# A narrower odd matmul for each token pair, its mirror on VectorE and its sum on GpSimd a slot ahead

## The chip, the cores and the metric

The kernel runs on one core of a Trainium2 chip. The metric is the device time of one execution in microseconds; the median of three runs is 424.52 us (424.30 to 424.62).

## The reference

The input x is 8 x 3072 x 256 (f32). It goes through a Fourier mixing (the real part of an FFT over the sequence and the channels) and then through a feed-forward layer whose hidden unit is the maximum of three linear maps:

```python
X = np.fft.fft(np.fft.fft(x, axis=1), axis=2).real          # 8 x 3072 x 256
t = X.reshape(24576, 256)
h = np.maximum(np.maximum(t @ w1, t @ w2), t @ w3)          # 24576 x 768
out = h @ w_out                                              # 24576 x 256, f32
```

The matmuls of the kernel take bf16 and sum in f32.

## The kernel before

**The mathematics used.** The real part of a Fourier transform of real data splits into an even and an odd part, and the tokens come in pairs whose even parts agree and whose odd parts differ in sign (but for one channel row). So each mixed batch is kept as two bf16 matrices, `tE` and `tO`, of 128 rows and 1536 token pairs. One pair yields two tokens, called plus and minus here. The maximum of three maps is written as `w1` plus the larger of two differences and zero, so that the output has a linear part, `tE` and `tO` times the small matrices in `gw`, and a hidden part, `hp` (plus) and `hm` (minus) times `wout_bf`.

**Units.** For each of B = 8 batches there are three blocks of 512 token pairs (`blk`), and in each block six units (`jc`, 128 hidden columns each): 18 units a batch (`UNITS`). A unit does this in program order, and each engine runs its own instructions in that order:

- `unit_plus`: four 512-column matmuls into two PSUM banks (lines 476, 477); `unit_out` evicts them, ScalarE with a relu into `stmp` (line 490) and VectorE with a maximum into `hp` (line 491).
- `finish` of the unit before: `unit_minus`, two 512-column matmuls into that unit's banks (line 484), and again the two evictions, into `hm`. The banks of a unit are thus free two units later.
- `l2_some(10)`: ten steps of the second layer of the block before. A step is one `next()` of a generator, which runs up to its next `yield`, as a rule one matmul.
- the planned pieces of that unit (`plan`): the mixing of the next batch (`s` and `k` pieces, lines 430 to 460), the fetches of x by SyncE's queue, and the casts of x on GpSimd (`turn_chunk`, lines 144 and 146).

After the six units `l2_some(1000)` runs what is left of the generator.

**The second layer.** `l2_block` handles four slots of 128 token pairs. For every two slots the even part goes into a bank `pl` (two 256-column matmuls, line 516) and ScalarE copies it to `even` (line 520). For each slot a bank `po` gets the odd part of both tokens, one 512-column matmul against 512 columns of `gw` (line 524, followed by a second `yield`), then six 256-column matmuls of `hp` in its left half and six of `hm` in its right half (line 500). VectorE then adds the even part to both halves and writes `ot` (line 529). A GpSimd indirect DMA stores the minus half (line 534), SyncE the plus half (line 544). `po` comes from the pool `ps_o`, which has two buffers: slot s+2 takes the bank of slot s once everything that reads it is done. There are 23 such blocks, 92 slots; the last block of the last batch has a function of its own, `l2_last`.

**The weights.** `prep_second` (called through `prep_some`) computes `gw` in unit 5 of the first batch: twelve matmuls into `psw`, a cast by VectorE (line 409) and a scaled copy by ScalarE (line 410).

Of the kernel before, what the change touches and what calls it, by code (L numbers as in the profile page):

```python
# [9 lines left out]
FP32 = mybir.dt.float32  # L10
BF16 = mybir.dt.bfloat16
INT32 = mybir.dt.int32
AX = mybir.ActivationFunctionType
ALU = mybir.AluOpType
# [19 lines left out]
def kernel(  # L34
# [46 lines left out]
    gE = [consts.tile([128, DFF], BF16, name=f"gE{i}", tag=f"gE{i}") for i in range(2)]  # L81
    gO = [consts.tile([128, DFF], BF16, name=f"gO{i}", tag=f"gO{i}") for i in range(2)]
    gD = [consts.tile([128, DFF], BF16, name=f"gD{i}", tag=f"gD{i}") for i in range(2)]
    gw = consts.tile([128, 768], BF16, tag="gw")
    rows_m = consts.tile([128, 12 * B], INT32, tag="rows_m")
    mark = consts.tile([1, 1], FP32, tag="mark")
    sgn = consts.tile([128, 1], FP32, tag="sgn")
    dif = consts.tile([128, 1], FP32, tag="dif")
    t_mid = consts.tile([128, 2, B], BF16, tag="t_mid")
    z_all = consts.tile([128, 128 * 26], BF16, tag="z_all")  # L90
    z = z_all.rearrange("p (c r) -> p c r", r=26)
# [40 lines left out]
                     in_=bass.AP(xs.tensor, xs.offset + (m - 1) * 64 + lo,  # L132
                                 [xs.ap[0], [1, hi - lo], [-64, m]]))

    def turn_chunk(b, ch):

        if ch == 0:
            x0 = x0_pool.tile([96, 66 * 130], BF16, name="x0", tag="x0")
            v = x0.rearrange("p (dl bb) -> p dl bb", bb=130)
            turned[b] = (lambda d: v[:, d, 0:128], rows_back(v[:, 33:66, :]))  # L140
            turned[b, "v"] = v
        v = turned[b, "v"]
        xs = raw.pop((b, ch))
        nc.gpsimd.tensor_copy(v[:, 0:33, ch * 32:ch * 32 + 32],  # L144
                              xs[:, 0:32 * 64].rearrange("p (bb dl) -> p dl bb", dl=64)[:, 0:33, :])
        reverse(lambda out, in_: nc.gpsimd.tensor_copy(out, in_), v[:, 33:66, :], xs,  # L146
                ch * 32, 33 if ch == 3 else 32)

    def rows_back(v):
        return lambda d: v[:, 32 - d, 0:128] if d else v[:, 32, 1:129]  # L150
# [60 lines left out]
    for (name, value) in (("half_pi", 0.5 * math.pi), ("rnd", ROUND), ("n24", -24.0)):  # L211
        c = gen.tile([128, 1], FP32, name=name, tag=name)
        nc.vector.memset(c, value)
        consts_of[name] = c
    nc.vector.memset(z[:, :, 24:26], 0.0)
    nc.vector.memset(m0f[:, 50:52], 0.0)
    nc.vector.memset(m0r[:, 50:52], 0.0)
    half = gen.tile([128, 256], FP32, tag="half")
# [169 lines left out]
    def prep_second():  # L388

        for jp in range(NJC // 2):  # L390
            pst = ps_f.tile([128, 512], FP32, name="pst", tag="ps")
            for k in range(2):
                jc = jp * 2 + k
                for fc in range(2):
                    nc.tensor.matmul(
                        pst[:, k * 256:(k + 1) * 256],
                        w1_bf[:, fc * DFF + jc * 128: fc * DFF + jc * 128 + 128],
                        md[fc], start=(fc == 0), stop=(fc == 1))
            nc.vector.tensor_copy(out=g1t[:, jp * 512:(jp + 1) * 512], in_=pst)
            yield  # L400
        psw = ps_f.tile([128, 512], FP32, name="psw", tag="ps")
        for half in range(2):
            for jc in range(NJC):
                nc.tensor.matmul(
                    psw[:, half * 256:(half + 1) * 256],
                    g1t[:, jc * 256 + half * 128: jc * 256 + half * 128 + 128],
                    wout_bf[:, jc * 256:(jc + 1) * 256],
                    start=(jc == 0), stop=(jc == NJC - 1))
        nc.vector.tensor_copy(out=gw[:, 0:512], in_=psw)
        nc.scalar.activation(out=gw[:, 512:768], in_=psw[:, 256:512], func=AX.Copy, scale=sgn)  # L410
        yield

    class Mix:
# [87 lines left out]
                             start=False, stop=(jc == NJC - 1), skip_group_check=True)  # L501
            yield

    def l2_block(b, blk, hp, hm, te, to):

        base = b * S
        for sub in range(4):
            slot = blk * 4 + sub
            r = slot + 1
            cp = slice(slot * 128, slot * 128 + 128)  # L510
            sp = slice(sub * 128, sub * 128 + 128)
            if sub % 2 == 0:
                pl = ps_f.tile([128, 512], FP32, name="pl", tag="ps")
                for i in range(2):
                    ci = (slot + i) * 128
                    nc.tensor.matmul(pl[:, i * 256:(i + 1) * 256], te[:, ci:ci + 128],  # L516
                                     gw[:, 0:256], start=True, stop=True)
                    yield
                even = even_pool.tile([128, 512], FP32, name="even", tag="even")
                nc.scalar.copy(out=even, in_=pl)  # L520
            lin = even[:, (sub % 2) * 256:(sub % 2 + 1) * 256]
            po = ps_o.tile([128, 512], FP32, name="po", tag="po")
            ot = out_pool.tile([128, 512], FP32, name="ot", tag="ot")
            nc.tensor.matmul(po, to[:, cp], gw[:, 256:768], start=True, stop=True)  # L524
            yield
            yield
            yield from l2_hidden(po[:, 0:256], lambda jc: hp[:, jc, sp])
            yield from l2_hidden(po[:, 256:512], lambda jc: hm[:, jc, sp])
            nc.vector.tensor_tensor(  # L529
                out=ot.rearrange("p (h c) -> p h c", h=2),  # L530
                in0=po.rearrange("p (h c) -> p h c", h=2),
                in1=lin.unsqueeze(1).to_broadcast([128, 2, 256]), op=ALU.add)
            lo = 1 if r == 12 else 0
            stored(nc.gpsimd.indirect_dma_start(  # L534
                out, bass.IndirectOffsetOnAxis(
                    ap=rows_m[0:128 - lo, b * 12 + slot: b * 12 + slot + 1], axis=0),
                ot[lo:128, 256:512], None), "scattered", ("scattered", "direct"))
            nc.gpsimd.memset(mark, 0.0)
            if r <= 11:
                stores = [(0, 128, base + r)]  # L540
            else:
                stores = [(0, 64, base), (64, 128, base + 12)]
            for (p0, p1, row) in stores:
                stored(nc.sync.dma_start(out=out[row: row + 24 * (p1 - p0 - 1) + 1: 24, :],
                                         in_=ot[p0:p1, 0:256]), "direct", ("scattered",))

    def l2_last(hp, hm, te, to, flipped):
# [3 lines left out]
        for sub in (3, 0, 1, 2):  # L551
# [6 lines left out]
            ot = out_pool.tile([128, 512], FP32, name="ot", tag="ot")  # L558
            for (h, tev, tov, wo, hid) in (
                    (0, te[:, cp], to[:, cp], gw[:, 256:512], lambda jc: hp[:, jc, sp]),  # L560
                    (1, ter[:, sm], tor[:, sm], gw[:, 512:768], lambda jc: hm[:, jc, sm])):
                if sub == 2 and h == 1:
                    po = ps_f.tile([128, 512], FP32, name="pol", tag="ps")
                ph = po[:, h * 256:(h + 1) * 256]
                nc.tensor.matmul(ph, tev, gw[:, 0:256], start=True, stop=False)
                yield
                nc.tensor.matmul(ph, tov, wo, start=False, stop=True)
                yield
                yield from l2_hidden(ph, hid)
                if sub == 2:  # L570
                    nc.vector.tensor_copy(out=ot[:, h * 256:(h + 1) * 256], in_=ph)
# [72 lines left out]
    ps_o = ctx.enter_context(tc.tile_pool(name="ps_o", bufs=2, space=bass.MemoryType.PSUM))  # L644
    h_pool = ctx.enter_context(tc.tile_pool(name="hbuf", bufs=2))
    out_pool = ctx.enter_context(tc.tile_pool(name="outbuf", bufs=6))
    even_pool = ctx.enter_context(tc.tile_pool(name="evenbuf", bufs=2))
    second = [prep_first(1, lambda: ps_o.tile([128, 512], FP32, name="psg", tag="po")),
              prep_second()]

# [17 lines left out]
    def at(b, unit, fn):  # L668
        plan.setdefault((b + unit // UNITS, unit % UNITS), []).append(fn)
# [16 lines left out]

    for (u, fn) in ((0, prep_some), (0, prep_some), (1, prep_some), (1, prep_some),
                    (2, lambda: m.k(2)), (2, prep_some), (3, lambda: m.k(3)),
                    (3, prep_some), (4, prep_some), (5, prep_some),
                    (6, lambda: m.k(4)), (7, lambda: m.k(5)), (7, m.end),  # L690
                    (0, lambda: turn_chunk(1, 0)), (2, lambda: turn_chunk(1, 1)),
                    (5, lambda: turn_chunk(1, 2)), (8, lambda: turn_chunk(1, 3))):
        at(0, u, fn)
    for ch in range(4):
        at(0, (6, 7, 9, 11)[ch], lambda ch=ch: fetch(2, ch))
    for b in range(B - 1):
        for i, whats in enumerate(ahead):
            for what in whats:
                at(b, begin[b] + i - (b == 0 and i >= 6), lambda b=b, what=what: piece(b + 1, what))
        if b + 2 < B:  # L700
            folds = begin[b] + 8 if b else 14
            for ch in range(4):
                at(b, folds + (0, 2, 4, 6)[ch], lambda b=b, ch=ch: turn_chunk(b + 2, ch))
                if b + 3 < B:
                    at(b, UNITS + (0, 1, 2, 4)[ch], lambda b=b, ch=ch: fetch(b + 3, ch))

    for b in range(B):
# [15 lines left out]
        for blk in range(3):  # L723
# [7 lines left out]
            for jc in range(NJC):  # L731
# [2 lines left out]
                if prev is not None:  # L734
                    finish(prev)
                prev = (pses, tO[:, cs], jc, hm)
                l2_some(10)
                if b == B - 1 and blk == 0:
                    if jc == 0:
                        middle = l2_mid()  # L740
# [5 lines left out]
            if blk == 2:  # L746
                finish(prev)
            l2_queue.append(l2_last(hp, hm, tE, tO, flipped) if b == B - 1 and blk == 2 else
                            l2_block(b, blk, hp, hm, tE, tO))

    l2_some(1000)

# [28 lines left out]
```

## Time and profile before

| | |
|---|---|
| median of three runs | 424.52 us |
| the profiled execution | 424.57 us, span of the engines 422.8 us |
| granted TensorE clock | 1.00 |
| PE busy | 404.0 us (96%) |
| VectorE (DVE) busy | 276.8 us (65%) |
| ScalarE (ACT) busy | 258.9 us (61%) |
| GpSimd (POOL) busy | 243.8 us (58%) |
| one batch in steady state | 48.45 us (18 units) |

All times are of one execution. A line of the timeline gives the start and the length in us, the engine, the source line, the operation, the output and the inputs, and in brackets how long the engine had been idle and what ended that. A line of the groups gives the count, the busy time in us, the mean length in ns, and the idle time ahead with its cause. Matmuls are pipelined: the length of one is longer than the time to the start of the next, and the spacing of starts is what PE spends on it.

### The profile page before, as it was taken

The numbers are of one execution on the slowest core, as the hardware profiler recorded it, in microseconds if no ns is written. First come the engines' busy times: TensorE is split into PE (matmuls) and PEld (weight loads), VectorE is DVE, ScalarE is ACT, GpSimd is POOL, SyncE is SP. The second block draws the span as 40 slices with busy tenths as digits, with TensorE's granted clock in tenths as the row PEclk, the third lists the DMA queues.
The fourth block names the chain that finished last, engine by engine and source line by source line (L and its number), as shares of the span: only waits on it lengthen the run. The fifth ranks groups of instructions, "written<-read, shape, count | busy, mean of one in ns | idle before, by whom it ended". The sixth has DMA issues, their size and how long they took to land.

```text
span 422.8 us, 8683 instructions
## 1 busy us (share of the span) xinstructions
PE 404.0 (96%) x3028; PEld 270.1 (64%) x3083; DVE 276.8 (65%) x460; ACT 258.9 (61%) x478; POOL 243.8 (58%) x291
## 2 busy tenths in 40 slices
PE   0899999999999999999999999999999999999996
PEld 0365667666676766666676666666666666666665
DVE  8877666566666665675666665675656665666773
ACT  6856666666665666556666666656665566655650
POOL 9927837962479526982299525983289621214420
PEclk9999999999999999999999999999999999999999
DMA  9998895793318831596217841387211221212213
GB/s 107 105 181 179 181 219 143 166 205 85 107 66 204 182 129 43 130 222 125 98 61 187 201 135 51 111 203 174 98 64 64 64 76 64 75 51 54 98 73 128
DMA packets 131172, 51.89 MB, mean 123 GB/s; under 512 B 113073, under 2 KB 128184, under 8 KB 131128
## 3 DMA queue, kind: packets, MB, share of 16 engines
q1 hardware_dynamic: 105408, 35.93, 35.8%
q0 software_dynamic: 24784, 15.08, 16.5%
q8 instruction: 24, 0.39, 0.4%
q10 hardware_dynamic: 936, 0.33, 0.3%
q14 instruction: 20, 0.16, 0.1%
HBM read 29.02 MB, written 25.17 MB: 128 GB/s over the span
## 4 chain that ended last, share of the span: by engine, by line
PE 87%; POOL 4%; DVE 3%; issue 3%; ACT 2%; DMA 1%; DVEq 0%; ACTq 0%; POOLq 0%
PE po L500 28%; PE pse L476 15%; PE pse L484 13%; PE pse L477 12%; PE po L524 4%; POOL x L100 3%; PE ps L458 2%; PE ps L456 2%; PE ps L430 2%; PE pl L516 2%; PE ps L432 2%; ACT stmp L490 1%; DVE ot L529 1%; PE psg L376 1%; DVE hp L491 1%
## 5 line engine op out<-in xcount | busy, mean ns | idle before, releaser
L490 ACT ACTIVATE stmp<-pse 128x512 bf16<-128x512 f32 x288 | 171.6, 600 | 52.0 <-PE pse L477 38.6
L534 POOL DMA_INDIRECT out_dram<-ot,rows_m x92 | 100.3, 1090 | 157.8 <-DVE ot L529 149.7
L491 DVE TENSOR_TENSOR hp<-pse,stmp 128x512 bf16<-128x512 f32 x144 | 99.6, 691 | 126.8 <-ACT stmp L490 87.0
L476 PE MATMUL pse<-t,gE 128*128 128x512 bf16 x285 | 108.1, 379 | 2.2 <-ACT t L460 0.2
L491 DVE TENSOR_TENSOR hm<-pse,stmp 128x512 bf16<-128x512 f32 x144 | 99.2, 689 | 6.8 <-ACT stmp L490 6.7
L477 PE MATMUL pse<-t,gO 128*128 128x512 bf16 x255 | 96.6, 379 | 0.2
L500 PE MATMUL po<-wout_bf,hp 128*128 128x256 bf16 x576 | 86.1, 273 | 0.3
L484 PE MATMUL pse<-t,gD 128*128 128x512 bf16 x274 | 82.7, 379 | 0.4
L500 PE MATMUL po<-wout_bf,hm 128*128 128x256 bf16 x570 | 77.8, 273 | 0.3
L500 PEld LDWEIGHTS <-hp 128*128 128x128 bf16 x576 | 56.3, 98 | 26.2
L500 PEld LDWEIGHTS <-hm 128*128 128x128 bf16 x576 | 56.4, 98 | 16.3
L144 POOL CAST x<-xs 96x1056 bf16<-96x1056 f32 x28 | 56.8, 2028 | 11.0 <-DMA xs<-in_x_dram 11.0
L529 DVE TENSOR_TENSOR ot<-po,even 128x512 f32<-128x512 f32 x92 | 62.9, 684 | 0.0
L146 POOL CAST x<-xs 96x1056 bf16<-96x1056 f32 (+1 forms) x35 | 58.2, 1675 | 0.0
L460 ACT CAST t<-ps 128x512 bf16<-128x512 f32 x47 | 27.5, 585 | 43.3 <-PE ps L458 43.2
L437 ACT CAST z_all<-ps 128x480 bf16<-128x480 f32 x45 | 25.1, 558 | 42.1 <-PE ps L432 42.1
L484 PEld LDWEIGHTS <-gD 128*128 128x128 bf16 x288 | 27.9, 98 | 32.2
L477 PEld LDWEIGHTS <-gO 128*128 128x128 bf16 x288 | 28.1, 98 | 20.3 <-issue 1.5
L476 PEld LDWEIGHTS <-gE 128*128 128x128 bf16 x288 | 28.1, 98 | 19.2 <-issue 0.4
L524 PE MATMUL po<-gw,t 128*128 128x512 bf16 x87 | 33.0, 379 | 0.0
L520 ACT COPY even<-pl 128x512 f32<-128x512 f32 x46 | 26.8, 582 | 0.1
L430 PE MATMUL ps<-m24f,x 96*128 96x96 bf16 x224 | 24.7, 205 | 0.0
(147 smaller groups left out, 328.2 us busy)
## 6 DMA issues: line engine op xcount, KB each, us to landing
xs<-in_x_dram SPq DMA_DIRECT2D x84, 198.0 KB
out_dram<-ot SPq DMA_DIRECT2D x90, 128.0 KB
xs<-in_x_dram SPq DMA_DIRECT2D x28, 192.0 KB
out_dram<-ot,rows_m POOLq DMA_INDIRECT x92, 3.3
x<-in_x_dram POOLq DMA_DIRECT2D x12, 96.0 KB, 4.3
w_bf<-in_moe_w_dram POOLq DMA_DIRECT2D x6, 192.0 KB, 5.5
out_dram<-ot SPq DMA_DIRECT2D x17, 64.0 KB
xs<-in_x_dram SPq DMA_DIRECT2D x32, 5.8 KB
```

The costliest lines, as they stand in the source:

```text
L144: nc.gpsimd.tensor_copy(v[:, 0:33, ch * 32:ch * 32 + 32], xs[:, 0:32 * 64].rearrange("p (bb dl) -> p dl bb", dl=64)[:, 0:33, :])
L146: reverse(lambda out, in_: nc.gpsimd.tensor_copy(out, in_), v[:, 33:66, :], xs, ch * 32, 33 if ch == 3 else 32)
L430: nc.tensor.matmul(ps1[:, c0:c0 + n], x0[0](d), mf[:, 0:n], start=True, stop=False)
L476: nc.tensor.matmul(pse[:, 0:n], gE[i][:, js], te, start=True, stop=False)
L477: nc.tensor.matmul(pse[:, 0:n], gO[i][:, js], to, start=False, stop=True)
L484: nc.tensor.matmul(pse, gD[i][:, js], to, start=False, stop=True, skip_group_check=True)
L490: nc.scalar.activation(out=stmp[:, 0:n], in_=pses[0][:, 0:n], func=AX.Relu)
L491: nc.vector.tensor_tensor(out=dst, in0=src3, in1=stmp[:, 0:n], op=ALU.max)
L500: nc.tensor.matmul(po, hcols(jc), wout_bf[:, jc * 256:(jc + 1) * 256], start=False, stop=(jc == NJC - 1), skip_group_check=True)
L524: nc.tensor.matmul(po, to[:, cp], gw[:, 256:768], start=True, stop=True)
L529: nc.vector.tensor_tensor(out=ot.rearrange("p (h c) -> p h c", h=2), in0=po.rearrange("p (h c) -> p h c", h=2), in1=lin.unsqueeze(1).to_br ...
L534: stored(nc.gpsimd.indirect_dma_start(out, bass.IndirectOffsetOnAxis(ap=rows_m[0:128 - lo, b * 12 + slot: b * 12 + slot + 1], axis=0), ot[ ...
```

## The change

The odd part of a slot is computed for the plus token alone: one matmul of 257 columns, 256 of weights and one that picks row 0 of `tO`. The odd part of the minus token is its negative, but for row 0, which enters with the same sign. VectorE makes this mirror: `other = twice * po[:, 256] - po[:, 0:256]`, where `twice` holds twice the weights' row 0 (with 1 subtracted in column 0, because column 256 of the bank also stays under the minus half). GpSimd adds the even part and leaves a line of 512 values, even | even + other; VectorE's last sum takes it as it is. Even part, odd matmul, mirror and GpSimd's add of a slot are issued while the slot before is being worked on: the odd part between its `hp` and its `hm` matmuls, the even part of a pair between the third and the fourth `hp` matmul of an odd slot. The second `yield` is gone, and `l2_some` takes 10, 9, 9, 10, 9, 9 steps in the units of a block. A new piece of `prep_second` makes `twice` (one matmul, two VectorE operations) and takes a planned place of its own in unit 5. The casts of x are cut into halves (17 and 16 of 33 columns `d`), one to a unit in units 6 to 21 (in batch 0 two to a unit, 14 to 21). `even` has three buffers of double width in place of two.

```diff
@@ turn_chunk
+        for (d0, d1) in (((0, 17), (17, 33))[part % 2:part % 2 + 1] if part is not None else ((0, 33),)):
+            if part is None or part < 2:
+                nc.gpsimd.tensor_copy(v[:, d0:d1, ch * 32:ch * 32 + 32],
+                                      xs[:, 0:32 * 64].rearrange("p (bb dl) -> p dl bb", dl=64)[:, d0:d1, :])
+            if part is None or part >= 2:
+                reverse(lambda out, in_: nc.gpsimd.tensor_copy(out, in_), v[:, 33:66, :], xs,
+                        ch * 32, 33 if ch == 3 else 32, 32 + d0, 32 + d1)
@@ start
+    nc.vector.memset(two_row, 0.0)
+    nc.vector.memset(two_row[0:1], 2.0)
+    nc.vector.memset(gw[:, 512:513], 0.0)
+    nc.vector.memset(gw[0:1, 512:513], 1.0)
@@ prep_second
         nc.vector.tensor_copy(out=gw[:, 0:512], in_=psw)
-        nc.scalar.activation(out=gw[:, 512:768], in_=psw[:, 256:512], func=AX.Copy, scale=sgn)
+        nc.scalar.activation(out=gw[:, 514:770], in_=psw[:, 256:512], func=AX.Copy, scale=sgn)
+        yield
+        pst = ps_f.tile([128, 512], FP32, name="pst", tag="ps")
+        nc.tensor.matmul(pst[:, 0:256], two_row, gw[:, 256:512], start=True, stop=True)
+        nc.vector.tensor_copy(out=twice, in_=pst[:, 0:256])
+        nc.vector.tensor_scalar(out=twice[:, 0:1], in0=twice[:, 0:1], scalar1=-1.0, scalar2=None,
+                                op0=ALU.add)
         yield
@@ second layer
+    def l2_even(b, slot):
+        pl = ps_f.tile([128, 512], FP32, name="pl", tag="ps")
+        for i in range(2):
+            ci = (slot + i) * 128
+            nc.tensor.matmul(pl[:, i * 256:(i + 1) * 256], mixes[b].tE[:, ci:ci + 128],
+                             gw[:, 0:256], start=True, stop=True)
+            yield
+        even = even_pool.tile([128, 1024], FP32, name="even", tag="even")
+        nc.scalar.copy(out=even.rearrange("p (i c) -> p i c", i=2)[:, :, 0:256],
+                       in_=pl.rearrange("p (i c) -> p i c", i=2))
+        for i in range(2):
+            lines[b, slot + i] = even[:, i * 512:(i + 1) * 512]
+
+    def l2_odd(b, slot):
+        po = ps_o.tile([128, 512], FP32, name="po", tag="po")
+        nc.tensor.matmul(po[:, 0:257], mixes[b].tO[:, slot * 128:slot * 128 + 128], gw[:, 256:513],
+                         start=True, stop=True)
+        other = other_pool.tile([128, 256], FP32, name="other", tag="other")
+        nc.vector.scalar_tensor_tensor(out=other, in0=twice, scalar=po[:, 256:257],
+                                       in1=po[:, 0:256], op0=ALU.mult, op1=ALU.subtract)
+        line = lines[b, slot]
+        nc.gpsimd.tensor_tensor(out=line[:, 256:512], in0=line[:, 0:256], in1=other, op=ALU.add)
+        odd[b, slot] = po
+        yield
@@ l2_block
-            po = ps_o.tile([128, 512], FP32, name="po", tag="po")
-            nc.tensor.matmul(po, to[:, cp], gw[:, 256:768], start=True, stop=True)
-            yield
-            yield
-            yield from l2_hidden(po[:, 0:256], lambda jc: hp[:, jc, sp])
+            if (b, slot) not in odd:
+                yield from l2_even(b, slot)
+                yield from l2_odd(b, slot)
+            after = (b, slot + 1) if slot < 11 else (b + 1, 0)
+            lin = lines.pop((b, slot))
+            po = odd.pop((b, slot))
+            first = l2_hidden(po[:, 0:256], lambda jc: hp[:, jc, sp])
+            for _ in range(3):
+                next(first)
+                yield
+            if after < (B - 1, 8) and sub % 2:
+                yield from l2_even(*after)
+            yield from first
+            if after < (B - 1, 8):
+                yield from l2_odd(*after)
             yield from l2_hidden(po[:, 256:512], lambda jc: hm[:, jc, sp])
-            nc.vector.tensor_tensor(
-                out=ot.rearrange("p (h c) -> p h c", h=2),
-                in0=po.rearrange("p (h c) -> p h c", h=2),
-                in1=lin.unsqueeze(1).to_broadcast([128, 2, 256]), op=ALU.add)
+            nc.vector.tensor_tensor(out=ot, in0=po, in1=lin, op=ALU.add)
@@ plan
-                    (3, prep_some), (4, prep_some), (5, prep_some),
+                    (3, prep_some), (4, prep_some), (5, prep_some), (5, prep_some),
...
             for ch in range(4):
-                at(b, folds + (0, 2, 4, 6)[ch], lambda b=b, ch=ch: turn_chunk(b + 2, ch))
+                for part in range(4):
+                    at(b, 6 + 4 * ch + part if b else 14 + 2 * ch + part // 2,
+                       lambda b=b, ch=ch, part=part: turn_chunk(b + 2, ch, part))
@@ unit loop
-                l2_some(10)
+                l2_some(9 + (jc % 3 == 0))
```

More of the change, by code (lines that the diff above doesn't have):

```diff
@@ L83 @@
     gD = [consts.tile([128, DFF], BF16, name=f"gD{i}", tag=f"gD{i}") for i in range(2)]
-    gw = consts.tile([128, 768], BF16, tag="gw")
+    gw = consts.tile([128, 770], BF16, tag="gw")
     rows_m = consts.tile([128, 12 * B], INT32, tag="rows_m")
     mark = consts.tile([1, 1], FP32, tag="mark")
+    two_row = consts.tile([128, 128], BF16, tag="two_row")
     sgn = consts.tile([128, 1], FP32, tag="sgn")
     dif = consts.tile([128, 1], FP32, tag="dif")
+    twice = consts.tile([128, 256], FP32, tag="twice")
     t_mid = consts.tile([128, 2, B], BF16, tag="t_mid")
@@ L133, in reverse, with turn_chunk @@
                                  [xs.ap[0], [1, hi - lo], [-64, m]]))
-    def turn_chunk(b, ch):
-        if ch == 0:
+    def turn_chunk(b, ch, part=None):
+        if (b, "v") not in turned:
             x0 = x0_pool.tile([96, 66 * 130], BF16, name="x0", tag="x0")
@@ L142, in turn_chunk @@
         v = turned[b, "v"]
[L143 to L147, printed above, removed]
+        xs = raw[b, ch]
+        for (d0, d1) in (((0, 17), (17, 33))[part % 2:part % 2 + 1] if part is not None else ((0, 33),)):
[5 more added lines that the diff above has]
+                        ch * 32, 33 if ch == 3 else 32, 32 + d0, 32 + d1)
     def rows_back(v):
@@ L502, in l2_hidden, with l2_block @@
             yield
-    def l2_block(b, blk, hp, hm, te, to):
+    lines = {}
+    odd = {}
+    def l2_even(b, slot):
[21 more added lines that the diff above has]
+        yield
+    def l2_block(b, blk, hp, hm):
         base = b * S
@@ L509, in l2_block @@
             r = slot + 1
-            cp = slice(slot * 128, slot * 128 + 128)
             sp = slice(sub * 128, sub * 128 + 128)
[L512 to L517, printed above, removed]
-                    yield
-                even = even_pool.tile([128, 512], FP32, name="even", tag="even")
-                nc.scalar.copy(out=even, in_=pl)
-            lin = even[:, (sub % 2) * 256:(sub % 2 + 1) * 256]
-            po = ps_o.tile([128, 512], FP32, name="po", tag="po")
-            ot = out_pool.tile([128, 512], FP32, name="ot", tag="ot")
-            nc.tensor.matmul(po, to[:, cp], gw[:, 256:768], start=True, stop=True)
-            yield
-            yield
-            yield from l2_hidden(po[:, 0:256], lambda jc: hp[:, jc, sp])
+            if (b, slot) not in odd:
[4 more added lines that the diff above has]
+            po = odd.pop((b, slot))
+            ot = out_pool.tile([128, 512], FP32, name="ot", tag="ot")
+            first = l2_hidden(po[:, 0:256], lambda jc: hp[:, jc, sp])
[7 more added lines that the diff above has]
+                yield from l2_odd(*after)
             yield from l2_hidden(po[:, 256:512], lambda jc: hm[:, jc, sp])
-            nc.vector.tensor_tensor(
-                out=ot.rearrange("p (h c) -> p h c", h=2),
-                in0=po.rearrange("p (h c) -> p h c", h=2),
-                in1=lin.unsqueeze(1).to_broadcast([128, 2, 256]), op=ALU.add)
+            nc.vector.tensor_tensor(out=ot, in0=po, in1=lin, op=ALU.add)
             lo = 1 if r == 12 else 0
@@ L560, in l2_last @@
                     (0, te[:, cp], to[:, cp], gw[:, 256:512], lambda jc: hp[:, jc, sp]),
-                    (1, ter[:, sm], tor[:, sm], gw[:, 512:768], lambda jc: hm[:, jc, sm])):
+                    (1, ter[:, sm], tor[:, sm], gw[:, 514:770], lambda jc: hm[:, jc, sm])):
                 if sub == 2 and h == 1:
@@ L646 @@
     out_pool = ctx.enter_context(tc.tile_pool(name="outbuf", bufs=6))
-    even_pool = ctx.enter_context(tc.tile_pool(name="evenbuf", bufs=2))
+    other_pool = ctx.enter_context(tc.tile_pool(name="otherbuf", bufs=2))
+    even_pool = ctx.enter_context(tc.tile_pool(name="evenbuf", bufs=3))
     second = [prep_first(1, lambda: ps_o.tile([128, 512], FP32, name="psg", tag="po")),
@@ L700 @@
         if b + 2 < B:
-            folds = begin[b] + 8 if b else 14
             for ch in range(4):
-                at(b, folds + (0, 2, 4, 6)[ch], lambda b=b, ch=ch: turn_chunk(b + 2, ch))
+                for part in range(4):
+                    at(b, 6 + 4 * ch + part if b else 14 + 2 * ch + part // 2,
+                       lambda b=b, ch=ch, part=part: turn_chunk(b + 2, ch, part))
                 if b + 3 < B:
@@ L748 @@
             l2_queue.append(l2_last(hp, hm, tE, tO, flipped) if b == B - 1 and blk == 2 else
-                            l2_block(b, blk, hp, hm, tE, tO))
+                            l2_block(b, blk, hp, hm))
     l2_some(1000)
```

## The prediction

> **What bounds the kernel now.** I read the page first (busy times, slices), then the groups by form, then the timeline of one block in steady state and of the stage at 37 to 43 us, then GpSimd's own timeline.
>
> ```profile
> PE 404.0 (96%) x3028; PEld 270.1 (64%) x3083; DVE 276.8 (65%) x460; ACT 258.9 (61%) x478; POOL 243.8 (58%) x291
> ...
> PE   0899999999999999999999999999999999999996
> ...
> L534 POOL DMA_INDIRECT out_dram<-ot,rows_m x92 | 100.3, 1090 | 157.8 <-DVE ot L529 149.7
> L529 DVE TENSOR_TENSOR ot<-po,even 128x512 f32<-128x512 f32 x92 | 62.9, 684 | 0.0
> ```
>
> PE is never idle after the first 20 us; every other engine has a third of its time free. So a matmul cycle saved is time saved, and a wait put in front of a matmul is time lost in full. The timeline around one unit (four `unit_plus`, two `unit_minus`, then a group of `l2_some` steps, then a planned piece) shows how the engines stand to each other:
>
> ```profile
> 243.48 0.82 PE L500 MATMUL po<-wout_bf,hm 128*128 128x256 bf16 x6
> ...
> 244.56 0.81 PE L476 MATMUL pse<-t,gE 128*128 128x512 bf16 x2
> ...
> 245.42 0.59 PE L484 MATMUL pse<-t,gD 128*128 128x512 bf16 x2
> 245.85 0.69 DVE L491 TENSOR_TENSOR hp<-pse,stmp 128x512 bf16<-128x512 f32 x1 [1.50 <-ACT stmp L490]
> 245.85 0.38 PE L516 MATMUL pl<-gw,t 128*128 128x256 bf16 x2
> ...
> 246.07 0.38 PE L524 MATMUL po<-gw,t 128*128 128x512 bf16 x1
> 246.29 0.82 PE L500 MATMUL po<-wout_bf,hp 128*128 128x256 bf16 x6
> ...
> 246.47 0.69 DVE L491 TENSOR_TENSOR hm<-pse,stmp 128x512 bf16<-128x512 f32 x1
> ...
> 247.08 0.68 DVE L529 TENSOR_TENSOR ot<-po,even 128x512 f32<-128x512 f32 x1
> ```
>
> Three things. A 512-column matmul holds PE 0.22 us (246.07 to 246.29), a 256-column one 0.11 (245.85 to 246.07). With T = 244.56 the unit's l2 steps start at T+1.29. And the sum into `ot` (L529) is late: its last matmul started at 244.03 (243.48 plus five times 0.109), yet it runs at T+2.52 to T+3.20. A generator emits what follows its last yield only at the next call, and when a slot ends on the last step of a group, that call is in the next unit, behind that unit's `hp` and `hm` on VectorE. VectorE was idle 1.50 us meanwhile. Today nobody needs that bank soon: the next slots use the other one.
>
> **The change, part by part.**
>
> Odd part. 92 matmuls go from 512 to 257 columns: 92 x (0.2155 - 0.1095) = 9.75 us off PE.
>
> Steps. A block of l2 now has 56 steps, one matmul each: slot 0 has 13 (odd of slot 1 at step 6), slot 1 steps 13 to 27 (odd of slot 2 at 21), slot 2 steps 28 to 40 (odd of slot 3 at 34), slot 3 steps 41 to 55 (odd of the next block's slot 0 at 49). The groups of 10, 9, 9, 10, 9, 9 take steps 0-9, 10-18, 19-27, 28-37, 38-46, 47-55. Four odd matmuls and four first `hp` matmuls are thus in different units, so the new wait of `hp` for VectorE's mirror is covered: mirror at T+2.52 to T+2.94, `hp` no earlier than the next unit's T+1.29, that is T+3.56 in the shortest unit (6 x 0.2155 + 9 x 0.109 = 2.27 us). Without that cover it would cost about 1 us a slot.
>
> The bank. `ps_o` has two buffers, so odd of slot s+1 overwrites the bank of slot s-1 and must wait for `ot` of s-1. For steps 6, 21 and 49 that `ot` runs half a microsecond or more ahead (the tightest: `ot` of slot 0 ends at T+3.21 of unit 1, odd at T+3.78). For step 34 it doesn't. Slot 1 ends on step 27, the last of the third group, so its `ot` comes out with step 28, in the fourth unit, at T+2.52 to T+3.20 as in the timeline. Odd of slot 3 is due six steps into the same unit: T + 1.29 + 6 x 0.109 = T+1.95. From VectorE's end to PE's start takes 0.05 us in the nearest row (below: `hm` ends at 38.22, the matmul into its bank starts at 38.27), 0.14 at the start (`nat` to PE at 20.12). So PE stands still 3.25 - 1.95 = 1.30 us (1.4 with the longer release), in every block of l2_block: 23 of them. In the first, three extra steps put odd at T+2.27: 0.98. Sum 22 x 1.30 + 0.98 = 29.6 us. Nothing covers it, PE being in order.
>
> The start. The new `pst` matmul stands right behind `psw` and reads `gw`:
>
> ```profile
> 37.53 0.69 DVE L491 TENSOR_TENSOR hm<-pse,stmp 128x512 bf16<-128x512 f32 x1
> ...
> 38.27 0.38 PE L476 MATMUL pse<-t,gE 128*128 128x512 bf16 x1
> ...
> 40.45 0.38 PE L476 MATMUL pse<-t,gE 128*128 128x512 bf16 x1
> ...
> 40.65 0.69 DVE L409 CAST gw<-psw 128x512 bf16<-128x512 f32 x1 [0.21 <-PE psw L404]
> ```
>
> `gw` is done at 41.34; today PE goes on at 40.45, with it at 41.40 + 0.11 = 41.51: 1.06 lost. Slot (0,0) has its mirror and its `hp` in one group: `hm` and mirror end at T+2.94, `hp` is due at T+1.62: 1.37 lost. Together 2.4 us; zero to 3 are the ends. Four memsets (0.06 to 0.17 each) on VectorE ahead of the first loads: 0.1.
>
> VectorE. The mirror (`scalar_tensor_tensor`, 256 columns out of PSUM) isn't in the trace: 425 ns for a 256-column copy out of PSUM (L571) below, 684 for L529 above; nearest the first: 0.42, 39 us in all, in its free third. With 0.68 the units with mirror and `ot` would run 0.2 late, some 2 us over the kernel.
>
> GpSimd. The add of two 128x256 f32 isn't there either. Casts of 1056 and 32 columns (2035 and 234 ns) give 0.18 + 1.76 ns a column: 0.63 for one input of 256, 1.08 for two; the bf16 copy of 512 in 609 gives a lower end near 0.3. I take 0.8. [...] Of a batch's 12 slots GpSimd then has 16 half casts at 1.1 (17.6 plus 0.5 for the short pieces), 12 stores at 0.97 + 0.17 gap, one of them 1.6 longer (15.3), memsets 1.1 and adds 9.6: 44 of the new 51 us (48.45 - 1.28 + 3 x 1.30). It has over 4 us between mirror and need. Batch 0 packs two casts a unit into units 14 to 21; there it falls behind about 4 us, at the edge: 0.2 us, up to 1. Queued behind a late add is `ot` on VectorE, and behind that all `hp`; that is the price if the cover goes.
>
> The spread casts and the strided `even` copy change no wait: x is fetched in a batch's units 0 to 4, the DMA engines are back under half load 25 us after the first fetch (246 of 221 us), and its casts stand in units 6 to 21, each chunk's 14 us or more behind its fetch.
>
> Sum, against the profiled execution's 424.57 (span 422.8, and within 0.05 of the median): 424.57 - 9.75 + 29.6 + 2.4 + 0.1 + 0.2 = 447.1.
>
> **Rivals.** (1) The bank is free in time, because `ot` of slot 1 is emitted a step earlier than I count or the bank's release isn't where I see it. Then 447.1 - 29.6, and with shorter blocks GpSimd's lag in batch 0 costs some 1.2 and VectorE's margins 0.5: 419. It decides by one step: at 27 steps or fewer for the first two slots the sum runs within the third unit, T+2.87 to T+3.56, before odd at the fourth's T+1.95 (= T+4.22). For it speaks that no matmul waits for L529 today; against it that L534's 149.7 us of waiting come from exactly these late sums. Chance 0.13. (2) GpSimd binds: from an add of (51 - 34.5) / 12 = 1.38 us on, each 0.1 more costs 1.2 us a batch for six batches; at 1.6 it gives 447 + 16 = 463. Above my upper end: 0.04. (3) The stalls make PE slow afterwards. At the start PE's first 27 matmuls last 479 ns on average, later ones of that size 379; at such a price after each of 23 stalls, 23 x 27 x 0.1 = 62 us: 509. The granted clock reads 1.00 through the stops at 24 to 42 us; 0.02. [...] (4) 257 columns cost as 512: 457; against it the spacing of 0.042 at 96, 0.109 at 256, 0.216 at 512. 0.02.
>
> **Numbers.** Forecast 447.1, chance 0.79, own range 443.5 to 451.5 (release 0.05 to 0.14, start 0 to 3, mirror and add at their ends). For eight in ten I put 442 to 454. Slower by over 0.2% (about what a measurement of this kernel can tell): 0.79 + 0.04 + 0.02 + 0.02 = 0.87; faster 0.12 from rival 1; 0.01 between.
>
> **What would show it.** In the profile after: about 23 PE stops of 1.0 to 1.4 us, three a batch, each before the 257-column matmul and ended by VectorE's `ot`, some 30 us in the waits; PE busy near 394 us, a batch in about 51 us rather than 48.45; 1.1 us of PE waiting for `gw` near 41 us and 1.4 for the first mirror; POOL adds under 1.1 us. Wrong if PE has no such stops, if `ot` of slot 1 runs before the fourth unit's `hp`, or if the stops stand before `hp` matmuls instead.

## The result and the profile after

| | median, us | ratio to before |
|---|---|---|
| before | 424.59 | |
| after | 455.03 (454.5 to 457.4) | 1.0719 (1.0705 to 1.0733) |
| forecast | 447.1, range 442 to 454 | |

The change makes the kernel slower, as forecast, but by 30.4 us and not by 22.5; the time lies 1 us above the range. The profiled execution is the slowest of the five (457.38 us, span 455.6). Its page, first the busy times, PE's slices and the clock granted to PE in each slice (tenths), then the groups that answer to those shown of before, with the odd matmul added:

```profile
PE 404.8 (89%) x3084; PEld 270.9 (59%) x3084; DVE 313.4 (69%) x558; ACT 259.4 (57%) x478; POOL 317.1 (70%) x431
...
PE   0779889889889889889889889889889889889886
...
PEclk9979999999999999999999999999999999999999
...
L575 POOL DMA_INDIRECT out_dram<-ot,rows_m x92 | 103.2, 1122 | 82.7 <-DVE ot L573 75.1
...
L573 DVE TENSOR_TENSOR ot<-po,even 128x512 f32<-128x512 f32 x92 | 62.6, 681 | 3.1 <-POOL even L545 2.8
...
L539 PE MATMUL po<-gw,t 128*128 128x257 bf16 x92 | 25.3, 275 | 27.3 <-DVE ot L573 27.3
```

PE's slices run 9, 8, 8 to the end: two 8s in every three slices of 11.4 us, which is two blocks of 17 us, so a stop comes back with every block. The last group names it: PE waits 27.3 us ahead of the 257-column matmul, for `ot`. The second and third slices are 7s, and in the third the granted clock reads 7 tenths: the start is slower as well. (PE's busy time doesn't fall to the 394 us of the forecast: a stop counts as idle only from the modelled end of the matmul ahead, 0.16 us after the next could start, part of the start runs at half the clock (0.50 from 25 to 30 us), and 55 of before's records of matmuls were missing.)

The timeline of the unit that holds the stop answers to the one shown of before:

```profile
250.72 0.38 PE L491 MATMUL pse<-t,gE 128*128 128x512 bf16 x1
...
251.98 0.69 DVE L506 TENSOR_TENSOR hp<-pse,stmp 128x512 bf16<-128x512 f32 x1 [0.55 <-PE pse L499]
252.01 0.82 PE L515 MATMUL po<-wout_bf,hp 128*128 128x256 bf16 x6
...
252.62 0.69 DVE L506 TENSOR_TENSOR hm<-pse,stmp 128x512 bf16<-128x512 f32 x1
253.23 0.68 DVE L573 TENSOR_TENSOR ot<-po,even 128x512 f32<-128x512 f32 x1
253.97 0.28 PE L539 MATMUL po<-gw,t 128*128 128x257 bf16 x1 [1.14 <-DVE ot L573]
254.09 0.49 PE L515 MATMUL po<-wout_bf,hm 128*128 128x256 bf16 x3
```

T is 250.72. The six `hp` matmuls start at T+1.29; the odd matmul of slot 3 is due at 252.66 (T+1.94) and starts at 253.97, 0.06 us behind the end of slot 1's `ot` (253.91): 1.31 us lost. The bracket says 1.14, because it counts from the modelled end of the last `hp` matmul. One batch takes 51.13 us (first `hp` of batch 4 at 245.66, of batch 5 at 296.79).

The start, VectorE's timeline, before and then after. Before:

```profile
12.26 1.11 DVE L131 COPY back<-x 96x1056 bf16<-96x1056 bf16 x1
```

After:

```profile
18.76 1.15 DVE L133 COPY back<-x 96x1056 bf16<-96x1056 bf16 x1 [3.91 <-DMA x<-in_x_dram]
```

The first x arrives late, and the first unit's `hp` runs at 36.02 us where it ran at 27.73. PE's timeline shows two losses on the way. The first matmuls of the mixing, before:

```profile
20.12 0.20 PE L430 MATMUL ps<-m24f,nat 96*128 96x96 bf16 x1 [0.15 <-DVE nat L316]
20.16 0.20 PE L432 MATMUL ps<-m24r,back 96*128 96x96 bf16 x1
```

And after:

```profile
26.14 0.24 PE L445 MATMUL ps<-m24f,nat 96*128 96x96 bf16 x1 [5.64 <-DVE nat L325]
...
26.26 0.28 PE L445 MATMUL ps<-m24f,nat 96*128 96x96 bf16 x1
26.34 0.28 PE L447 MATMUL ps<-m24r,back 96*128 96x96 bf16 x1
```

PE waits 5.64 us for the copies of x and starts the mixing 6.0 us later. Then it goes at half its pace, 0.08 us a matmul instead of 0.042, up to 30.9 us: the clock granted from 25 to 30 us is 0.50, where it was 1.00. That is the other 2.3 us of the 8.3. No step of the forecast had either loss. The change doesn't touch the loads of x, but its new tiles stand among the constants, ahead of the tiles of x: in the built program the first tile of x lies at byte 62464 of a partition before (a multiple of 512) and at 63776 after (32 past a multiple of 256).

### The profile page after: what moved, and what is told of

Read it like the earlier page. It is cut to its first block, busy times and chain, and to the rows that moved or that the text cites. A ratio compares the mean times of both kernels' runs of the same rounds, so it can differ in the third digit from the quotient of the medians.

```text
span 455.6 us, 9096 instructions
## 1 busy us (share of the span) xinstructions
PE 404.8 (89%) x3084; PEld 270.9 (59%) x3084; DVE 313.4 (69%) x558; ACT 259.4 (57%) x478; POOL 317.1 (70%) x431
## 4 chain that ended last, share of the span: by engine, by line
PE 66%; DMA 9%; issue 6%; DVE 6%; SPq 5%; ACT 4%; POOL 4%; DVEq 0%; ACTq 0%; POOLq 0%
PE po L515 21%; PE pse L491 11%; PE pse L492 10%; PE pse L499 10%; DMA xs<-in_x_dram 6%; SPq L102 5%; DVE ot L573 4%; ACT stmp L505 3%; PE po L539 3%; DMA x<-in_x_dram 2%; PE pl L527 2%; PE ps L445 2%; PE ps L447 2%; PE ps L473 2%; PE ps L471 2%
## 5 line engine op out<-in xcount | busy, mean ns | idle before, releaser
L575 POOL DMA_INDIRECT out_dram<-ot,rows_m x92 | 103.2, 1122 | 82.7 <-DVE ot L573 75.1
L492 PE MATMUL pse<-t,gO 128*128 128x512 bf16 x288 | 109.0, 379 | 0.0
L515 PE MATMUL po<-wout_bf,hp 128*128 128x256 bf16 x576 | 93.0, 273 | 1.3 <-DVE other L542 1.3
L499 PE MATMUL pse<-t,gD 128*128 128x512 bf16 x288 | 85.6, 379 | 0.0
L515 PE MATMUL po<-wout_bf,hm 128*128 128x256 bf16 x570 | 85.3, 273 | 0.0
L545 POOL TENSOR_TENSOR even<-even,other 128x256 f32<-128x256 f32 x92 | 66.7, 725 | 22.2 <-DVE other L542 18.8
L148 POOL CAST x<-xs 96x544 bf16<-96x544 f32 (+2 forms) x52 | 60.5, 1168 | 19.4 <-DMA xs<-in_x_dram 19.4
L151 POOL CAST x<-xs 96x544 bf16<-96x544 f32 (+5 forms) x59 | 62.0, 1061 | 0.0
L542 DVE SCALAR_TENSOR_TENSOR other<-twice,po 128x256 f32<-128x256 f32 x92 | 44.0, 478 | 9.7 <-PE po L539 9.7
L539 PE MATMUL po<-gw,t 128*128 128x257 bf16 x92 | 25.3, 275 | 27.3 <-DVE ot L573 27.3
L491 PEld LDWEIGHTS <-gE 128*128 128x128 bf16 x288 | 28.1, 98 | 21.1 <-issue 2.4
L492 PEld LDWEIGHTS <-gO 128*128 128x128 bf16 x288 | 28.1, 98 | 20.6 <-issue 1.9
```

What stands on the lines that cost most here:

```text
L148: nc.gpsimd.tensor_copy(v[:, d0:d1, ch * 32:ch * 32 + 32], xs[:, 0:32 * 64].rearrange("p (bb dl) -> p dl bb", dl=64)[:, d0:d1, :])
L491: nc.tensor.matmul(pse[:, 0:n], gE[i][:, js], te, start=True, stop=False)
L492: nc.tensor.matmul(pse[:, 0:n], gO[i][:, js], to, start=False, stop=True)
L499: nc.tensor.matmul(pse, gD[i][:, js], to, start=False, stop=True, skip_group_check=True)
L515: nc.tensor.matmul(po, hcols(jc), wout_bf[:, jc * 256:(jc + 1) * 256], start=False, stop=(jc == NJC - 1), skip_group_check=True)
L542: nc.vector.scalar_tensor_tensor(out=other, in0=twice, scalar=po[:, 256:257], in1=po[:, 0:256], op0=ALU.mult, op1=ALU.subtract)
```

## The experiments

Two theories: the stop is the bank of slot 1, freed late because its `ot` is emitted a call too late; and the late start is the place of the tiles. Rivals: the mirror causes the stops; the start is late for another reason. In the tables "first `hp`" is the start of the first unit's `hp`, and q1 and q0 (the queues of SyncE and of GpSimd) are the page's share times the span: the time their packets held the 16 engines.

**The place of the tiles.** One unused tile among the constants, of 32 or 224 bytes in the changed kernel, of 32, 128 or 256 in the kernel before:

```diff
     t_mid = consts.tile([128, 2, B], BF16, tag="t_mid")
+    spare = consts.tile([128, N // 4], FP32, tag="spare")
```

> The changed kernel with one unused tile of 32 bytes a partition among the constants, so that the tiles of x and of the output lie at multiples of 64 bytes again, as before the change (the change moved them by 1312 bytes, to 32 past such a multiple). Theory A (transfers to and from tiles 32 bytes off a multiple of 64 are slower, and that delays the first x): the first unit starts near 28 us as in the kernel before, not 36; queue q1 falls from 201 us of engine time back to about 151; time near 447. Rival B (the first loads are slow for another reason, the added memsets or the state of the chip): nothing changes, 455.

> As the run with 32 bytes, but with 224, which puts the first tile of x at a multiple of 512 bytes. If a multiple of 64 is what matters: the same time as with 32 bytes, near 447. If a coarser one (128 to 512) is: faster than with 32 bytes, which would lie between 447 and 455.

> The kernel before the change with 32 unused bytes among the constants, so that its tiles of x and of the output lie 32 past a multiple of 64 bytes; nothing else differs. Theory A: the first unit starts some 8 us later and the time is about 433. Rival B: 424.6.

> The kernel before the change with 128 unused bytes among the constants: the tiles of x at 128 past a multiple of 256 bytes. The first x (rows of 128 bytes in SBUF, bf16) still lies within 256-byte lines, later x (rows of 256 bytes) straddles two. If straddling a 256-byte line is what costs: the first unit starts as before (near 28 us) or a little late, the time is 424.6 to 427, and queue q1 (x in f32) takes as long as with 32 bytes (about 196 us). If any multiple of 64 or 128 is good: 424.6 and q1 at 151. If what counts is only a multiple of 256 for any row: 431 as with 32 bytes.

> The same with 256 unused bytes, at multiples of 256 again but not of 512. If 256 is the line: 424.6, as the kernel before. If 512 is: near 431. If the loss comes with any shift of the tiles, and not with their alignment: 431 too.

| kernel | tiles of x, modulo 256 | time, us | first `hp` | q1, us | q0, us |
|---|---|---|---|---|---|
| before | 0 | 424.59 | 27.73 | 151 | 70 |
| before + 256 | 0 | 424.95 | 28.11 | 152 | 70 |
| before + 128 | 128 | 426.66 | 27.84 | 173 | 75 |
| before + 32 | 32 | 431.73 | 33.63 | 196 | 108 |
| after | 32 | 455.03 | 36.02 | 201 | 112 |
| after + 32 | 64 | 454.31 | 34.36 | 193 | 105 |
| after + 224 | 0 | 447.79 | 27.87 | 152 | 70 |

The queue lines of the page (packets, MB, share of the 16 engines) and the landing of the first loads (KB each, median us from issue to landing), after:

```profile
q1 hardware_dynamic: 105408, 35.93, 44.2%
q0 software_dynamic: 24784, 15.08, 24.6%
...
x<-in_x_dram POOLq DMA_DIRECT2D x12, 96.0 KB, 9.3
```

And with 224 bytes more:

```profile
q1 hardware_dynamic: 105408, 35.93, 34.1%
q0 software_dynamic: 24784, 15.08, 15.8%
...
x<-in_x_dram POOLq DMA_DIRECT2D x12, 96.0 KB, 4.3
```

The same packets and bytes take a quarter less time in q1 (152 us, not 201). So the place is the cause: 32 bytes alone make the kernel before 7.1 us slower (431.73 against 424.59), and 224 bytes give the changed kernel 7.2 us back. I expected 32 bytes to be enough there; a multiple of 64 is not (454.31 us), a multiple of 256 is (447.79). The kernel at 128 shows the two sorts of load apart: the first x, whose rows of 128 bytes lie between two multiples of 256, comes about as early as ever (first `hp` at 27.84, before at 27.73), while the rows of 256 bytes that SyncE fetches later lie across a multiple of 256 and q1 takes 22 us more (173, not 151). I expected about 196 us there, as with 32 bytes; it is 173. The queues carry the stores of `ot` too, whose tiles move alike, but most of the loss is in the loads: by the trace's packet records, q1's packets of 256 bytes took 111 us before, 129 with 128 bytes and 152 with 32, its packets of 1024 bytes 38, 42 and 41. In these runs a multiple of 256 is the line: with 256 bytes more, a multiple of 256 but not of 512, the kernel before keeps its time (424.95 us, q1 152). Off it, the offset of 128 costs less than that of 32 (q1 173 us against 196); why stays open. How the 7.1 us divide between late data and the lower clock that follows is read from the timelines, not tested: no run delays x as much and keeps the clock.

**The call in which `ot` is emitted.** The changed kernel, with the last sum and the stores in the step of the last `hm` matmul; matmuls, steps and groups are the same:

```diff
-            yield from l2_hidden(po[:, 256:512], lambda jc: hm[:, jc, sp])
+            second = l2_hidden(po[:, 256:512], lambda jc: hm[:, jc, sp])
+            for _ in range(5):
+                next(second)
+                yield
+            next(second)
             nc.vector.tensor_tensor(out=ot, in0=po, in1=lin, op=ALU.add)
 ...
+            yield        # after the stores
```

> The changed kernel with VectorE's last sum of a slot and its stores issued in the same step as the last hm matmul, not at the next call; steps, groups and matmuls are the same. Theory (the odd matmul of slot 3 waits for the sum of slot 1, which stands behind the next unit's evictions): the 24 stops of PE before the 257-column matmul go, some 27 us; 455 - 27 = 428, up to 431 if the units with mirror and sum now run VectorE late. Rival (the stops come from the mirror or from the shorter lead of the bank in general): they stay, 455.

426.94 us (ratio 1.0053, 1.0032 to 1.0075). PE's list of waits (us in total, times, longest):

```profile
PE ps L445 <- DVE nat L325: 3.8, 1, 3.8
PE po L515 <- DVE other L542: 1.3, 1, 1.3
PE po L539 <- DVE ot L577: 0.8, 1, 0.8
PE pst L422 <- DVE gw L418: 0.8, 1, 0.8
```

Of 24 waits for `ot` one is left, in the first block, whose steps are shifted by three; 28.1 us are won. The mirror isn't the cause of the others: it is still there, and they are gone. A batch takes 47.18 us (231.09 to 278.27), 1.27 less than before the change.

**Both repairs, and the start mended.** The first takes the early `ot` and 224 bytes together. The second also moves the `pst` matmul and the steps of the first block:

```diff
-                    (3, prep_some), (4, prep_some), (5, prep_some), (5, prep_some),
+                    (3, prep_some), (4, prep_some), (5, prep_some),
...
-                    (5, lambda: turn_chunk(1, 2)), (8, lambda: turn_chunk(1, 3))):
+                    (5, lambda: turn_chunk(1, 2)), (7, lambda: turn_chunk(1, 3))):
...
-                l2_some(9 + (jc % 3 == 0))
+                if (b, blk) == (0, 1):
+                    if jc == 0:
+                        prep_some()
+                    l2_some((3, 13, 10, 11, 7, 15)[jc])
+                else:
+                    l2_some(9 + (jc % 3 == 0))
```

> Both repairs: VectorE's last sum issued in the step of the last hm matmul, and 224 unused bytes among the constants, so that the tiles of x lie at multiples of 256 bytes. The two losses are at different places (the start; one stop a block), so they should add: 426.9 - (454.6 - 447.8) = about 420. If they overlap (less delay at the start is waited for elsewhere), 424 to 427.

> As the run with both repairs, and the start mended: the pst matmul stands behind the first unit's matmuls of block 1 and not in front of them, only the even and odd steps of the first slot are run in that unit (steps 3, 13, 10, 11, 7, 15 in place of 10, 9, 9, 10, 9, 9 in that block), and the last casts of batch 1 stand one unit earlier. By my sum the pst wait is 1.0, the first mirror 1.3 and the casts 0.5 us: 2.3 to 2.8 us less than the run with both repairs, about 417. If these stops only move other waits, no less than 419.5.

419.45 us (ratio 0.9876, 0.9860 to 0.9893) and 417.28 us (0.9829, 0.9811 to 0.9848): the losses add, and the last version beats the kernel before by 7.6 us. Of the start's stops it loses the one for `gw`, the one for the first mirror and the last one for `ot`; 1.0 us comes back as a wait of a `k` piece for the bank of `pl`, and the casts' 0.5 stay:

```profile
PE ps L472 <- ACT even L532: 1.0, 1, 1.0
...
PE ps L448 <- POOL x L152: 0.5, 1, 0.5
```

**What each part is worth, on the kernel with both repairs.** The odd matmul 512 columns wide again; the casts whole and in their old units; the sum on VectorE:

```diff
-        nc.tensor.matmul(po[:, 0:257], ..., gw[:, 256:513],
+        nc.tensor.matmul(po, ..., gw[:, 0:512],
-                for part in range(4):
-                    at(b, 6 + 4 * ch + part if b else 14 + 2 * ch + part // 2, ...)
+                at(b, folds + (0, 2, 4, 6)[ch], lambda b=b, ch=ch: turn_chunk(b + 2, ch))
-        nc.gpsimd.tensor_tensor(out=line[:, 256:512], in0=line[:, 0:256], in1=other, op=ALU.add)
+        nc.vector.tensor_tensor(out=line[:, 256:512], in0=line[:, 0:256], in1=other, op=ALU.add)
```

> The run with both repairs, with the odd matmul 512 columns wide again (against other columns of gw, so that the values of the linear part aren't the reference's; every wait and operation stays). By the spacing of 0.2155 against 0.1095 us: 92 x 0.106 = 9.75 us more, 429.2. If the matmuls were held by something else than their columns: 419.5.

428.02 us: 8.6 more where the columns alone give 9.75. PE's waits behind its first matmul come to 3.2 us in this trace and to 4.4 in the one compared with, which is about the difference; 0.6 of it is the wait for the first x, which owes nothing to the columns.

> The run with both repairs (419.45), with the casts of x whole and in the units where they stood before the change. My theory: GpSimd has room and VectorE's sum isn't late for its adds, so the halving and spreading is worth little: 419.5 to 420.5. Rival: two casts of 2.03 us in a row hold the add back past the need (a sum is due 2 units, some 5 us, behind the mirror) and PE stops: 422 or more, with waits of VectorE's ot for the add in the profile.

435.94 us, 16.5 more: my theory fell. The timeline shows the rival:

```profile
230.64 0.48 DVE L543 SCALAR_TENSOR_TENSOR other<-twice,po 128x256 f32<-128x256 f32 x1
...
232.65 2.02 POOL L149 CAST x<-xs 96x1056 bf16<-96x1056 f32 x1
...
234.62 2.00 POOL L152 CAST x<-xs 96x1056 bf16<-96x1056 f32 x1
...
236.58 0.72 POOL L546 TENSOR_TENSOR even<-even,other 128x256 f32<-128x256 f32 x1
237.34 0.69 DVE L578 TENSOR_TENSOR ot<-po,even 128x512 f32<-128x512 f32 x1 [1.52 <-POOL even L546]
...
238.08 0.27 PE L540 MATMUL po<-gw,t 128*128 128x257 bf16 x1 [0.87 <-DVE ot L578]
```

The add of 236.58 belongs to the mirror of 230.64; GpSimd came to it only after an earlier add, the store and the 4 us of casts queued ahead. VectorE's sum waits 1.52 us for it, and PE for that sum's bank. There are ten such waits of VectorE, up to 3.3 us, 18.9 in all, and ten of PE, 10.7 in all. The lag is built up over three chunks in a row: it isn't one pair of casts that does it but GpSimd full from 218.8 to 237.3. The run changes two things at once, the halving and the units, so what each is worth stays open.

> The run with both repairs, with the sum even + other on VectorE in place of GpSimd, right behind the mirror. VectorE gets 92 more operations of 0.3 to 0.5 us, 28 to 45 us in all. My theory: the units with mirror, add and last sum have no room left (sum ends at T+3.56 without it, the next hp is due at T+3.53 in the short units), so PE loses 0.3 to 0.5 us in every second or third unit without a planned piece: 424 to 428. Rival: VectorE's idle time hides it, 419.5.

459.15 us, 39.7 more, far above what I expected. The group of the adds, then two of them with what GpSimd did:

```profile
L546 DVE TENSOR_TENSOR even<-even,other 128x256 f32<-128x256 f32 x92 | 103.9, 1130 | 3.4
```

```profile
68.29 0.42 DVE L546 TENSOR_TENSOR even<-even,other 128x256 f32<-128x256 f32 x1
...
76.52 4.13 DVE L546 TENSOR_TENSOR even<-even,other 128x256 f32<-128x256 f32 x1
```

```profile
76.11 2.15 POOL L149 CAST x<-xs 96x544 bf16<-96x544 f32 x2
78.20 2.17 POOL L152 CAST x<-xs 96x544 bf16<-96x544 f32 x2
```

Clear of the casts the add takes 0.42 us; started among them it ends at 80.65, just behind the last of them (80.37). Over the whole trace the adds that start during a cast end within 0.3 us of the end of that cast or of one right behind it. VectorE is 90% busy in this run, and PE waits for its evictions (26.1 us for `hm`, in 33 waits).

## Why the prediction was wrong, and where it was right

- **The bank: right, in place and size.** 23 stops, 22 of 1.30 and one of 0.98 us, were forecast; the trace has 1.31 in the unit shown and 0.97 in the first block (0.81 by the bracket). The profiled execution has a 24th, 1.29 us at 60.24, which isn't there with the tiles at a multiple of 256 bytes (23 waits). A batch was to be 51.07 us and is 51.13. Issuing `ot` earlier removes all but the one in the first block, and 28.1 us with them. Rival 1 (the bank free in time) is out. Its sum of 419 is near the time of the kernel with both repairs (419.45), in part by chance: that kernel keeps the first block's stop, and of the 1.7 us that the sum has for lags its trace shows 0.5, a wait for GpSimd's casts.
- **The odd part: right.** A batch without stops is 1.27 us shorter; 1.28 was the forecast.
- **The start: the step that failed.** It was given 2.4 us for `pst` and the first mirror, 0.1 for memsets, and took the loads of x as they were: the sum has no term for them, and no reason is given. The two stops are there (in the kernel with 224 bytes PE goes on at 41.65 where it would have at 40.60, 1.05 us against 1.06 forecast; the first mirror holds `hp` by 1.48, from 43.27 to 44.75, against 1.37). What was missing is that the change's tiles move every tile behind them by 1312 bytes, that x then lands slower, and that PE, which stands still for it, goes on at half the clock (0.50): 7.2 us in the medians. With the tiles at a multiple of 256 bytes, the changed kernel takes 447.79 us; the sum said 447.1.
- **VectorE and GpSimd: sizes off by little, one judgement by much.** The mirror takes 0.48 us (0.42 taken), the add 0.73 (0.8 taken). That GpSimd keeps up was right for the change as it stands. I argued it from the sum over a batch; what it rests on is that the casts are halved and spread, which the forecast passed over in a sentence and which is worth 16.5 us once the add is in that queue.
- **Rivals 2 to 4** didn't happen as they were put: the add is far under 1.38 us, matmuls behind a stop keep their 0.109 spacing (254.09 to 254.42 for three), and the 257-column matmul costs what its columns say (the next starts 0.11 us behind it, 278.89 to 279.00). But what rival 3 feared of the 23 short stops did happen once, behind the long one at the start that the forecast lacked.

## What to carry to other kernels

In a generator that hands out an engine's work in steps, what follows the last yield belongs to the next call; if it frees a bank, put it in the step before, and count in which group each release comes out and which matmul needs that bank next. When a change adds tiles, look where the tiles that DMA fills have moved: 32 bytes cost this kernel 7 us without any edit to its work. An in-order queue that is busy 72% of the time on average (GpSimd with the whole casts) can still be full where it matters (no gap over 0.2 us from 218.8 to 237.3); cut long items before putting a short, awaited one among them.

## What the runs showed of the hardware

- In these runs loads into SBUF with rows of 128 or 256 bytes took clearly longer when the tiles lay 32 or 64 bytes off a multiple of 256 (q1 151 to 196 us, q0 70 to 108 for the same packets, with 32 bytes in the kernel before; q1 193 and q0 105 at 64, with 32 bytes in the changed kernel, where a multiple of 256 has 152 and 70). With 32 bytes in the kernel before, the first loads land after 8.7 us instead of 4.3.
- The clock granted to PE fell with the long stops at the start: 0.50 from 25 to 30 us behind a stop of 5.64 (the change) or 3.77 (with the early `ot`), 0.71 behind one of 3.63 (32 bytes in the kernel before). Behind a stop of 1.23 (128 bytes in the kernel before) and behind the 1.3 us stops of the blocks it stayed at 1.00. Where between these it starts to fall was not tried.
- A VectorE add with both inputs in SBUF (0.42 us) took up to 4.13 us while GpSimd was casting, and ended just behind the casts; VectorE's sums with one input in PSUM (0.68) show none of this beside the same casts (mean 679 ns). Why the add waits for them was not shown. So GpSimd, though slower at an add (0.73 against 0.42), was the right place for this one: 419.45 us with the add there, 459.15 on VectorE.
